# Seven more matmuls on zeros, a Hankel tile loaded in half the partitions, and an earlier load of the output weights, in a fused attention and max-out feed-forward kernel

## The chip, the cores and the metric

The kernel runs on one core of one Trainium2 chip. The metric is the time of one execution in microseconds (us), as the device reports it. Three runs of the kernel before gave 312.24, 312.76 and 314.45 us; the median is 312.76 us.

## What is computed

Two operations are chained. The first is attention with a relative position bias, for 8 batches of 8 heads, 576 positions and 64 channels for each head. The second is a feed-forward block on the 4608 tokens of 512 channels that the attention gives. Its middle layer of 768 takes the largest of three products.

```python
scores = scale * np.matmul(q, k.transpose(0, 1, 3, 2))
bias = bias_table[bucket]                     # bucket depends on |i - j| alone, capped at 128
attn = softmax(scores + bias)                 # over the keys
x = (attn @ v) as 4608 tokens x 512           # heads side by side
h = np.maximum(np.maximum(x @ w1, x @ w2), x @ w3)
out = h @ w_out
```

## The kernel before, in words

**Units of work.** A batch has 576 positions: four tiles of 128 and a tail of 64. Heads are taken in pairs (`hp`, four pairs in a batch), since two heads of 64 channels fill 128 partitions. Queries are taken in two halves (`c` is 0 for queries 0 to 255, and 1 for 256 to 511), with the tails of queries and keys handled apart (`left_queries`, `left_keys`). For a pair, `scores` multiplies keys by queries into a PSUM tile `sc`, and ScalarE takes the exponential into `e4` in SBUF. The bias enters as a factor: `times_band` multiplies the part of `e4` that lies near the diagonal by a tile `hank` on VectorE. `attend` multiplies the result by the values `vx` (whose last column is ones, so that it gives the sums too), and its `quotients` divides on VectorE into `x_sb`. `x_sb` is transposed into `xT`, from which the feed-forward products are taken.

**The Hankel tile.** `spread_bias` makes, for each of the 8 heads, a row of 511 factors in `w_sb`, writes it to DRAM (`w_dr`), and `load_hank` reads it back so that partition p gets the row from element p on: 384 elements for each head, in two DMAs of four heads. `bandt` is a copy of a part of it for the tails.

**Order.** Nearly everything on TensorE, VectorE and ScalarE is put down in program order (`inorder`, with the helpers `mm`, `tr`, `dve_copy`, `act_copy`), so the order of the source lines is the order in each engine's queue. Feed-forward work waits in a list `pending` and is put between attention pieces by `fill`, in portions; `first`, `second` and `third` are the products with w1, w2 and w3 and are called `f`, `m` and `g` in the lists, and `o` is the output product with `wo_bf`.

**The first batch.** It is started by hand. Queries and keys come in as 32-bit values on the SP and ACT queues, or cast by DMA on the POOL queue, and are transposed on TensorE (`first_transposes` for keys and the first 256 queries, `more_transposes` for the other queries, `last_keys` for the key tails of pairs 0 and 1). While loads are on their way, TensorE multiplies a block of zeros: eight times at the very start (`warm`) and once in each head pair of the first half (`keep_warm`, tile `idle`). A first loop over `hp` does the first half of the queries of all four pairs, with the bands of pairs 0 and 1 at its end. A second loop does the other half, the attends, and the first feed-forward portions.

**The POOL queue.** All casting loads go through it, in program order: queries, keys and values of the first batch, w1, then in `load_second` the second batch and w2, the second batch's values, w3, then queries and keys of batch 2 (counted from 0), its values, the output weights `wo_bf`, and queries and keys of batch 3. Each such DMA also waits until the DMA eight places ahead of it has landed, since eight semaphores are used in turn. From batch 2 on, queries and keys are transposed by DMAs on the SP queue.

**Lines.** All matmuls have line 107 in the profile and all TensorE transposes line 111, since helpers record them; VectorE copies have 124, ScalarE copies 121, exponentials 777, band products 771, `w_sb` 306, the Hankel loads 313. A group is told apart by its tiles.

Of the kernel before, what the change touches and what calls it, by code (L numbers as in the profile page):

```python
# [39 lines left out]
def kernel(  # L40
# [12 lines left out]
    nc = tc.nc  # L53
# [52 lines left out]
    def mm(*args, **kw):  # L106
        made = inorder(nc.tensor.matmul(*args, **kw))  # L107
        return made
# [14 lines left out]
    def dve_copy(out_, in_):  # L123
        return inorder(nc.vector.tensor_copy(out_, in_))  # L124
# [22 lines left out]
    def in_turn(b, load):  # L147
        return inorder(load)
# [39 lines left out]
    def go_behind(loads, behind):  # L188

        for load in loads if behind else ():  # L190
            tc.add_manual_dep(
                load.ins, behind.ins.name,
                mybir.DependencyInfo(mybir.DependencyClass.Sync, mybir.DependencyReason.DATA),
                reason="these loads go behind the transposes in line",
            )

    def load_v(b, h0, h1, behind=None):
        loads = load_main(v, b, h0, h1, vx[b % 2][:, :, :, 0:D]) + load_tail(v, b, h0, h1, v_diag)
        go_behind(loads, behind)
        return loads[-1]  # L200
# [88 lines left out]


    warm = ps_s.tile([P, 2 * CH], F32, tag="sc", name="warm")
    for _ in range(8):
        mm(warm[:, 0:CH], lhsT=zeros[:, 0:P], rhs=zeros[:])

    act_copy(batch[0][0][:, 0:2, 0:2, :], q32[:, :, 0:2, :])
    w_sb = stage.tile([H, WL], BF16, name="w_sb")

    def spread_bias():
        spread = ps_a.tile([H, NW], F32, tag="a", name="spread")
# [7 lines left out]
        inorder(nc.scalar.dma_start(out=w_dr[:], in_=w_sb[:]))  # L307

    w_dr = dram.tile([H, WL], BF16, name="w_dr")
    hank = const.tile([P, H, BAND], BF16, name="hank")  # L310

    def load_hank(h0, h1):
        inorder(nc.sync.dma_start(
            out=hank[:, h0:h1, :],
            in_=bass.AP(
                tensor=w_dr.tensor, offset=w_dr.offset + h0 * WL,
                ap=[[1, P], [WL, h1 - h0], [1, BAND]],
            ),
        ))

# [43 lines left out]
    def ffn(t0, nt, last, tiled=False):  # L366
# [268 lines left out]
        if per == 1:  # L635
            portions = [[f[0], m[0]]]
            for fb in range(1, n_fb):
                portions.append([g[fb - 1], f[fb], m[fb]])
            portions.append([g[-1], (0, None), o[0]])
        else:  # L640
            if not t0:
                portions = [[f[0]], [m[0], f[1]], [m[1]], [f[2], m[2]]]
                deferred.append(([[g[0]], g[1:]], [[x] for x in o]))
                o = []
            else:
                portions = [x for gs, _ in deferred for x in gs]
                for fb in range(n_fb):
                    portions += [[f[fb], m[fb]], [g[fb]]]
                portions += [x for _, os in deferred for x in os] + [[o[0]]]
                o = o[1:]  # L650
# [61 lines left out]
    def first_transposes(hp):  # L712


        hs = slice(2 * hp, 2 * hp + 2)
        tp = ps_f.tile([P, 2 * CH], BF16, tag="ff", name="tp1")
        K, L = KT * P, KT * P + P
        tq = tp[:, L:] if hp else ps_f.tile([P, 2 * CH], BF16, tag="ff", name="tq1")
        for t in range(2):
            tr(tq[:, P * t : P * t + P], batch[0][0][:, t, hs, :].rearrange("p h d -> p (h d)"), ident[:])  # L720
        for t in range(KT):
            tr(tp[:, P * t : P * t + P], batch[0][1][:, t, hs, :].rearrange("p h d -> p (h d)"), ident[:])
        e = K if hp < 2 else L
        if e > K:
            tr(tp[:, K:L], ktail[0][:, hp, :], ident[:])
        dve_copy(qk[0][0][:, hp, 0:QS], tq[:, 0:QS])
        dve_copy(qk[0][1][:, hp, 0:e], tp[:, 0:e])
# [83 lines left out]
    def visit(qT, kT, e4, c, mid=None, el=None):  # L811

        if el is not None:
            banks = [ps_a.tile([P, KT * 64], F32, tag="a", name="scq") for _ in range(2)]
            turn_left_queries(qT, kT, banks)
            put_left_queries(el, banks)
        for tt in range(0, KT, 2):
            scores(qT, kT, e4, c, tt)
            if tt == 0 and mid:
                mid()  # L820
# [182 lines left out]
    cast_keys(0)  # L1003
    spread_bias()
    first_transposes(0)
    for h0 in (0, KT):
        load_hank(h0, h0 + KT)
    dve_copy(batch[0][0][:, 0:2, 2:KT, :], q32[:, :, 2:KT, :])
# [20 lines left out]
        load_v(1, 0, H)  # L1029
        load_w(2)  # L1030

    def load_last_weights(behind):
        load = in_turn(0, nc.gpsimd.dma_start(out=wo_bf[:], in_=moe_w_out.rearrange("(c p) m -> p c m", p=P)))
        go_behind([load], behind)

    def bands(hp):
        for t in range(KT):
            times_band(hp, first_e[hp], t, 0, QS, inorder)

    def keep_warm():  # L1040

        idle = ps_a.tile([P, CH], F32, tag="a", name="idle")
        mm(idle[:], lhsT=zeros[:, 0:P], rhs=zeros[:])


    first_e, lefts = [], []
# [1 line left out]
    for hp in range(HP):  # L1048
        qT, kT = (x[:, hp, :] for x in qk[0])
        e4, el = e_tiles()  # L1050
        first_e.append(e4)
        visit(qT, kT, e4, 0, (lambda: first_transposes(hp + 1)) if 0 < hp < HP - 1 else None)
        if hp == HP - 1:
            more_transposes(0)
        if hp == 0:
            first_transposes(1)
        if hp == 1:
            last_keys()
        if hp + 2 < HP:
            cast_keys(hp + 2)  # L1060
        if hp == HP - 1:
            bands(0)
            bands(1)
        late.append(lambda hp=hp, e4=e4, el=el: attend(0, hp, e4, el, 0))
        keep_warm()
        lefts.append(lambda hp=hp, qT=qT, kT=kT, el=el: left_keys(
            hp, qT, kT, el, 0, QS, ps_a.tile([P, QS], F32, tag="a", name="sct")
        ))
        while hp and lefts:
            lefts.pop(0)()  # L1070
# [9 lines left out]
    for hp in range(HP):  # L1080
        qT, kT = (x[:, hp, :] for x in qk[0])
        if begun:
            e4, el = begun.pop()
            more_transposes(hp + 1)
            scores(qT, kT, e4, 1, 2)
        else:
            e4, el = e_tiles()
            visit(qT, kT, e4, 1, (lambda: more_transposes(hp + 1)) if hp + 1 < HP else None)

        def keys():  # L1090
            left_keys(hp, qT, kT, el, QS, S)

        def queries():
            left_queries(hp, qT, kT, el)

        def late_bands(hp=hp, e4=e4):
            for t in range(KT):
                times_band(hp, e4, t, QS, QM, inorder)

        if hp == 0:  # L1100
            keys()
        if hp == 1:
            x_transposes(0, 0)
        quotients = next_late()
        if hp < 2:
            if hp == 0:
                make_bandt()
            quotients()
            if hp == 0:
                bands(2)  # L1110
            else:
                behind.pop()()
                keys()
            queries()
            if hp == 1:
                x_transposes(1, 0)
            else:
                begun.append(e_tiles())
                scores(*(x[:, 1, :] for x in qk[0]), begun[0][0], 1, 0)
            quotients = next_late()  # L1120
            quotients()
            if hp == 0:
                bands(3)
            behind.append(lambda late_bands=late_bands, hp=hp, el=el: (late_bands(), products(hp, el)))
        else:
            if behind:
                behind.pop()()
            if hp == 3:
                quotients()
                add_ffn(0, QS)  # L1130
                fill(8)
            keys()
            if hp == 2:
                quotients()
            queries()
            late_bands()
            if hp == 2:
                x_transposes(2, 0)
                x_transposes(3, 0)
            else:  # L1140
                batch[2] = load_tiles()
                load_qk(2)
                x_transposes(0, 1)
                fill(8, lambda: second_transposes(qk[1], 0))
            products(hp, el)
        late.append(lambda hp=hp, e4=e4, el=el: attend(0, hp, e4, el, 1))

    turned = [lambda hp=hp: x_transposes(hp, 1) for hp in range(1, HP)]
    for b, hp in [(b, hp) for b in range(1, B) for hp in range(HP)]:
# [132 lines left out]
        if hp == 1 and b > 1:  # L1282
            pending.extend((n, [fn]) for n, fn in rest)
            rest.clear()
            made, tail = ffn((b - 1) * CH, CH, False, [(b + (i + 2) // HP, (i + 2) % HP) >= ROWS for i in range(HP)])
        if hp == 2 and b + 1 < B:
            last_v = load_v(b + 1, 0, H, turned_qk[b + 1, 1, min(b, 2) if b < 4 else KT - 1])
            if b == 1:
                load_last_weights(turned_qk[2, 1, KT - 1])
                batch[3] = load_tiles()  # L1290
                load_qk(3, turned_qk[2, 1, KT - 1])
        if hp == 2 and 1 < b < B - 2:
# [73 lines left out]
```

## Time and profile before

| what | value |
|---|---|
| median of three runs | 312.76 us (312.24 to 314.45) |
| profiled execution | 312.26 us, of which 310.5 us lie between its first and last instruction |
| TensorE matmuls (PE) | busy 298.9 us, 96% of the span |
| ScalarE (ACT) | 202.4 us, 65% |
| VectorE (DVE) | 207.7 us, 67% |
| GpSimd (POOL) | 110.9 us, 36%, nearly all of it issuing DMAs |
| granted TensorE clock, mean | 0.989 |
| DMA | 40.48 MB in 163950 packets |

How to read it: times are from the start of the span. A row of the timeline has the start, the duration, the engine, the source line, the operation with its output and input tiles and shapes, a count, and in brackets how long the engine sat idle before and what ended the wait. A row of the table of windows has the bounds in us, the length, and for each engine the busy time and the number of instructions, then the granted TensorE clock (1.00 is full), the busy share of the DMA engines and GB/s. A DMA's landing is counted from its issue.

### The profile page before, as it was taken

What the parts mean: (1) busy time and instruction counts of PE and PEld (TensorE: products, weight loads), DVE (VectorE), ACT (ScalarE), POOL (GpSimd) and SP (SyncE); (2) the same over time, 40 slices, a digit from 0 to 9 for tenths busy, and PEclk for the clock granted to TensorE, in tenths of its full rate; (3) what the DMA queues carried; (4) which work ended last, traced back from release to release, by engine and by line L of the source; (5) the groups of instructions that cost most, each with busy time, mean ns of one, the idle gap of its engine ahead of it and who ended that gap; (6) DMA issues with size and microseconds to landing.
All of it is one profiled execution on the core that took longest, in us unless ns stands there. A gap on an engine that the chain in (4) does not pass through costs nothing.

```text
span 310.5 us, 10532 instructions
## 1 busy us (share of the span) xinstructions
PE 298.9 (96%) x4542; PEld 182.5 (59%) x4542; DVE 207.7 (67%) x475; ACT 202.4 (65%) x268; POOL 110.9 (36%) x147
## 2 busy tenths in 40 slices
PE   6989999999999999999999999989999999999995
PEld 2357777775555655657665756666667654444442
DVE  7389788776777776776777667766776665553552
ACT  3899988886778777767776877675776730122211
POOL 8978752951096008900647024901500000000000
PEclk9599999999999999999999999999999999999999
DMA  9999999999999999999999999999932014202003
GB/s 167 198 187 199 182 163 136 145 166 139 141 157 191 151 187 155 133 147 198 105 101 125 165 183 111 112 146 202 131 62 106 36 33 80 101 0 103 34 0 135
DMA packets 163950, 40.48 MB, mean 130 GB/s; under 512 B 153784, under 2 KB 159424, under 8 KB 163904
## 3 DMA queue, kind: packets, MB, share of 16 engines
q0 software_dynamic: 103840, 16.66, 75.7%
q1 hardware_dynamic: 58304, 22.69, 43.6%
q8 instruction: 35, 0.57, 0.8%
q10 hardware_dynamic: 1760, 0.47, 0.7%
q14 instruction: 11, 0.09, 0.1%
HBM read 35.39 MB, written 9.45 MB: 144 GB/s over the span
## 4 chain that ended last, share of the span: by engine, by line
PE 89%; ACT 5%; DMA 2%; issue 1%; DVE 1%; ACTq 1%; DVEq 0%
PE psp L107 34%; PE ps L107 19%; PE a L107 14%; PE sc L107 9%; PE pso L107 6%; ACT e L777 4%; PE sct L107 2%; PE scq L107 2%; PE tp L111 1%; DMA xT<-in_q_dram 1%; DMA out_dram<-osb 1%; ACT el L777 1%; ACTq L213 1%; PE xp L111 0%; DVE k_sb L124 0%
## 5 line engine op out<-in xcount | busy, mean ns | idle before, releaser
L777 ACT ACTIVATE e<-sc 128x1024 bf16<-128x1024 f32 x128 | 128.4, 1023 | 30.4 <-PE sc L107 27.3
L107 PEld LDWEIGHTS <-w_bf 64*128 64x128 bf16 (+1 forms) x1088 | 73.4, 95 | 57.9 <-issue 5.0
L107 PE MATMUL psp<-xT,w_bf 64*128 64x512 bf16 x736 | 91.9, 376 | 1.9 <-issue 1.8
L771 DVE TENSOR_TENSOR e<-e,hank 128x512 bf16<-128x512 bf16 (+2 forms) x136 | 62.3, 473 | 20.3 <-ACT e L777 19.7
L107 PE MATMUL ps<-xT,w_bf 128*128 128x512 bf16 (+1 forms) x352 | 65.6, 336 | 0.0
L153 POOL DMA_DIRECT2D vx<-in_v_dram x28 | 24.7, 895 | 83.0 <-DMA kT<-k_sb 40.7
L107 PE MATMUL sc<-qT,kT 64*128 64x256 bf16 (+1 forms) x384 | 48.6, 312 | 2.0 <-DVE kT L124 0.8
L107 PEld LDWEIGHTS <-kT 64*128 64x128 bf16 (+1 forms) x736 | 31.3, 95 | 26.8 <-issue 8.4
L107 PE MATMUL a<-vx,e 64*128 64x65 bf16 (+1 forms) x1536 | 44.7, 191 | 0.0
L107 PEld LDWEIGHTS <-e 64*128 64x128 bf16 (+1 forms) x1536 | 40.7, 95 | 3.7 <-issue 0.2
L107 PEld LDWEIGHTS <-hT 64*128 64x128 bf16 (+1 forms) x444 | 26.9, 95 | 19.4 <-DVE hT L519 1.9
L107 PE MATMUL a<-vt,el 64*128 64x65 bf16 (+1 forms) x240 | 30.8, 201 | 0.4 <-DVE m L484 0.4
L107 PEld LDWEIGHTS <-el 64*128 64x128 bf16 (+1 forms) x624 | 26.2, 95 | 7.9 <-issue 4.7
L394 ACT ACTIVATE m<-ps 128x512 bf16<-128x512 f32 x14 | 8.4, 597 | 34.3 <-PE ps L107 34.3
L777 ACT ACTIVATE el<-sct 128x576 bf16<-128x576 f32 (+2 forms) x36 | 21.6, 603 | 13.5 <-PE sct L107 13.1
L107 PE MATMUL psp<-wo_bf,hT 64*128 64x256 bf16 (+1 forms) x336 | 29.7, 307 | 0.0
L181 POOL DMA_DIRECT2D q_sb<-in_q_dram x24 | 22.1, 921 | 10.7 <-issue 4.6
L181 POOL DMA_DIRECT2D k_sb<-in_k_dram x24 | 22.0, 917 | 4.0 <-DMA wo_bf<-in_moe_w_out_dram 2.1
L107 PE MATMUL pso<-wo_bf,hT 128*128 128x512 bf16 (+2 forms) x108 | 23.2, 367 | 0.0
L777 ACT ACTIVATE el<-scq 128x512 bf16<-128x512 f32 (+1 forms) x33 | 19.2, 585 | 3.3 <-PE scq L107 3.2
L403 DVE TENSOR_TENSOR m<-ps,m 128x512 bf16<-128x512 f32 x14 | 9.7, 692 | 17.0 <-PE ps L107 17.0
L519 DVE TENSOR_TENSOR hT<-psp,m 128x1024 bf16<-128x1024 f32 x12 | 14.7, 1225 | 6.9 <-PE psp L107 6.9
(82 smaller groups left out, 287.6 us busy)
## 6 DMA issues: line engine op xcount, KB each, us to landing
out_dram<-osb SPq DMA_DIRECT2D x35, 256.0 KB, 2.8
vx<-in_v_dram POOLq DMA_DIRECT2D x28, 128.0 KB, 5.0
q_sb<-in_q_dram POOLq DMA_DIRECT2D x26, 128.0 KB, 7.6
k_sb<-in_k_dram POOLq DMA_DIRECT2D x24, 128.0 KB, 7.8
w_bf<-in_moe_w_dram POOLq DMA_DIRECT2D x3, 768.0 KB, 9.3
xT<-in_k_dram SPq DMA_DIRECT2D x6, 128.0 KB, 4.2
hank<-w_dr SPq DMA_DIRECT2D x2, 384.0 KB, 5.7
wo_bf<-in_moe_w_out_dram POOLq DMA_DIRECT2D x1, 768.0 KB, 8.8
```

The costliest lines, as they stand in the source:

```text
L107: made = inorder(nc.tensor.matmul(*args, **kw))
L111: inorder(nc.tensor.transpose(*args))
L153: in_turn(b, nc.gpsimd.dma_start(out=dst[:, t, h0:h1, :], in_=x[:, t, h0:h1, :])) for t in range(t0, t1)
L181: loads.append(in_turn(b, nc.gpsimd.dma_start(out=dst[:, t], in_=main_part(src, b)[:, t])))
L213: inorder(eng.dma_start(out=dst[:, :, h, :], in_=main_part(src, 0)[:, 0:nt, h, :]))
L394: nc.scalar.activation(out=st[fb]["m0"][:], in_=ps0, func=ACTF.Copy)
L403: inorder(nc.vector.tensor_tensor(out=m[:], in0=ps1, in1=st[fb]["m0"][:], op=ALU.max))
L519: return lambda: inorder(nc.vector.tensor_tensor(out=hT[:, fb * CH : fb * CH + 2 * CH].rearrange("p (i t) -> p i t", i=2), in0=ps2(), in1= ...
L771: put(nc.vector.tensor_tensor(out=e4[:, t, :, lo:hi], in0=e4[:, t, :, lo:hi], in1=hank[:, 2 * hp : 2 * hp + 2, c0:c1][:, :, ::-1], op=ALU. ...
L777: made = nc.scalar.activation(out=out_, in_=in_, func=ACTF.Exp, scale=inv_sqrt_d)
```

## The change

It joins several edits. (1) Seven matmuls on zeros are added: a ninth at the start, one between the first transposes and the first scores, one more in pairs 0, 1 and 3 of the first loop, and two in pair 0 of the second loop. (2) In the first loop the transposes of pair 2 come after the scores of pair 1 and no longer between their two halves. (3) In the first feed-forward portions, the second block's w1 product comes ahead of the first block's w2 product. (4) The Hankel tile is loaded into 64 partitions only, with 448 elements for each head, and two VectorE copies fill the other 64 partitions from it. The tile is 64 elements wider for each head, and `w_sb` now lies in a part of `xT` that is unused at that time. (5) The load of the output weights comes ahead of the third batch's values on the POOL queue, and no longer waits for a transpose of that batch.

```diff
-    for _ in range(8):
-        mm(warm[:, 0:CH], lhsT=zeros[:, 0:P], rhs=zeros[:])
+    def on_zeros(out_, n=1):
+        for _ in range(n):
+            mm(out_, lhsT=zeros[:, 0:P], rhs=zeros[:])
+
+    on_zeros(warm[:, 0:CH], 9)
...
-    w_sb = stage.tile([H, WL], BF16, name="w_sb")
+    w_sb = xT[0:H, 0, 3 * CH + P : 3 * CH + P + WL]
...
-    hank = const.tile([P, H, BAND], BF16, name="hank")
+    hank = const.tile([P, H, BAND + 64], BF16, name="hank")
...
-            out=hank[:, h0:h1, :],
+            out=hank[0:64, h0:h1, :],
...
-                ap=[[1, P], [WL, h1 - h0], [1, BAND]],
+                ap=[[1, 64], [WL, h1 - h0], [1, BAND + 64]],
...
+    def copy_hank(h0, h1):
+        dve_copy(hank[64:, h0:h1, 0:BAND], hank[0:64, h0:h1, 64:])
...
-                portions = [[f[0]], [m[0], f[1]], [m[1]], [f[2], m[2]]]
+                portions = [[f[0]], [f[1], m[0]], [m[1]], [f[2], m[2]]]
...
     first_transposes(0)
+    on_zeros(warm[:, 0:CH])
...
-    def load_last_weights(behind):
-        load = in_turn(0, nc.gpsimd.dma_start(out=wo_bf[:], in_=moe_w_out.rearrange("(c p) m -> p c m", p=P)))
-        go_behind([load], behind)
+    def load_last_weights():
+        in_turn(0, nc.gpsimd.dma_start(out=wo_bf[:], in_=moe_w_out.rearrange("(c p) m -> p c m", p=P)))
...
-    def keep_warm():
+    def keep_warm(n):
...
-        mm(idle[:], lhsT=zeros[:, 0:P], rhs=zeros[:])
+        on_zeros(idle[:], n)
...
-        visit(qT, kT, e4, 0, (lambda: first_transposes(hp + 1)) if 0 < hp < HP - 1 else None)
+        visit(qT, kT, e4, 0, (lambda: first_transposes(hp + 1)) if hp == 2 else None)
...
-        if hp == 0:
-            first_transposes(1)
+        if hp < 2:
+            first_transposes(hp + 1)
...
         if hp == HP - 1:
+            copy_hank(0, KT)
             bands(0)
             bands(1)
+            copy_hank(KT, H)
...
-        keep_warm()
+        keep_warm(1 if hp == 2 else 2)
...
         if hp == 0:
+            keep_warm(2)
             keys()
...
         if hp == 2 and b + 1 < B:
+            if b == 1:
+                load_last_weights()
             last_v = load_v(b + 1, 0, H, turned_qk[b + 1, 1, min(b, 2) if b < 4 else KT - 1])
             if b == 1:
-                load_last_weights(turned_qk[2, 1, KT - 1])
                 batch[3] = load_tiles()
```

## The prediction

> **What bounds the kernel now.** I read first the shares of the page: TensorE 96%, so a gain must give TensorE less idle or less slow time. The clock row of the page (9599...) has one low slice near the start, and all edits touch the first 70 us. So next I read windows around that slice, with bounds 3.41 us apart, since that spacing puts the low clock exactly into two of them.
>
> ```profile
> 4.07:7.48 3.41, 2.28 (x20) 0.88 (x18) 2.75 (x11) 1.64 (x5) 3.41 (x6) 1.00 1.57 210
> 7.48:10.89 3.41, 2.89 (x20) 1.37 (x20) 1.48 (x6) 2.69 (x3) 3.41 (x5) 0.50 2.08 179
> 10.89:14.30 3.41, 3.41 (x23) 1.37 (x22) 1.46 (x5) 2.71 (x4) 3.41 (x6) 0.50 1.22 208
> 14.30:17.71 3.41, 2.62 (x27) 1.23 (x26) 1.78 (x7) 3.37 (x6) 2.19 (x4) 1.00 2.09 181
> ```
>
> TensorE runs at half clock from 7.48 to 14.30. The window ahead of it has 2.28 us of matmul (67%); the one after, 2.62 us (77%), isn't followed by a drop. ACT is busy 2.7 of 3.41 us in the two slow windows and 3.37 in the next. Its timeline shows what the slow clock costs: three waits for scores, then a chain without a gap.
>
> ```profile
> 9.68 1.02 ACT L777 ACTIVATE e<-sc 128x1024 bf16<-128x1024 f32 x1 [0.53 <-PE sc L107]
> 11.08 1.02 ACT L777 ACTIVATE e<-sc 128x1024 bf16<-128x1024 f32 x1 [0.38 <-PE sc L107]
> 12.18 0.66 ACT L777 ACTIVATE el<-sct 128x256 bf16<-128x256 f32 x2
> 12.94 1.02 ACT L777 ACTIVATE e<-sc 128x1024 bf16<-128x1024 f32 x1
> 14.34 1.02 ACT L777 ACTIVATE e<-sc 128x1024 bf16<-128x1024 f32 x1 [0.38 <-PE sc L107]
> ```
>
> The chain of work that ended last agrees: PE and DVE up to 14.34, ACT exponentials to 18.72, then PE and ACT in turn, and PE nearly alone from 26.1 on. In the timeline VectorE sits idle 1.63 us before 16.12, then works almost without a gap to 30.8. Last I read which DMAs bound the way down.
>
> ```profile
> 17.36 0.70 POOL L223 DMA_DIRECT2D xT<-in_k_dram  x1 [1.22 <-DVE e L771]
> 20.74 0.79 POOL L1014 DMA_DIRECT2D w_bf<-in_moe_w_dram  x1
> 32.23 0.76 POOL L1014 DMA_DIRECT2D w_bf<-in_moe_w_dram  x1 [0.75 <-DMA xT<-in_k_dram]
> 57.96 0.85 POOL L1033 DMA_DIRECT2D wo_bf<-in_moe_w_out_dram  x1 [0.50 <-DMA kT<-k_sb]
> ```
>
> From issue to landing, w2 (20.74) and w3 (32.23) take 9.3 us each, so they land at 30.0 and 41.5; wo (57.96) takes 8.8 and lands at 66.8. In PE's timeline their first users start at 30.07, 41.87 and 68.62. So the slack is 0, 0.4 and 1.8 us: who speeds up the start runs into them. The key-tail transpose of batch 2 (issued 55.40, 6.0 to land: 61.4) has 0.9 us to its user at 62.31.
>
> **What the Trainium skill says.** "TensorE: Matmul & The Clock Gate", Part 1, has the clock at full or half only, set by how busy TensorE was in a free-running window of about 3.4 us, whose phase differs from run to run. The trace agrees: 0.50 for 6.82 us, two windows. The same page ("Wait — 56ns, not 53.3ns?") prices a 512-column matmul at 426.7 ns at half clock and 215.7 at full; here the starting zeros' weight loads are 0.43 us apart. "VectorE: DVE Perf Modes", the tier table, gives a bf16 SBUF copy the 4x rate; the trace agrees (64x768 in 350 ns, 128x512 in 279). "DMA: Bandwidth & Descriptors", "Queues, rings and completion order", says that an engine goes round between the queues that have work. The trace agrees: the first two value loads of batch 0, issued 0.76 us apart, land after 4.4 and 6.7 us, at 13.8 and 16.9; the Hankel loads (issued 10.01 and 10.38, landing after 5.2 and 6.2 us) lie between them. Later value loads land 0.3 to 0.5 us apart.
>
> **The change part by part.**
>
> *Zeros and order (1, 2).* Seven matmuls, 0.22 us each at full clock. Two fall into the window before the drop, into gaps in which TensorE waits for VectorE (0.47 us before 4.97, 0.52 before 6.52): they cost nothing and lift it from 2.28 to 2.71 us, 79%, over the 77% that was followed by full clock. So I take it that the clock stays up at 7.48. From there, step by step: pair 1's key transposes end 0.2 us earlier (0.39 instead of 0.60 us), its scores take 0.39 instead of 0.61, so its first exponential starts at 9.27 and not 9.68. Pair 1's second scores no longer stand behind seven transposes. ACT then runs at its own pace: 0.92 us for each exponential (1.83 for two, in the chain), 0.28 for each tail. 9.27 + 2 x 0.92 + 2 x 0.28 = 11.67; pair 2 to 13.51, its tail 13.79, pair 3 to 15.63. Before, pair 3's ended at 17.47. **ACT is 1.84 us ahead.** Moved transposes: pair 2's are 0.2 us of scores later, yet full clock ends them at 9.9 instead of 10.4. Inputs are there: queries' later tiles land by 11.1, tails by 11.6. The zeros after 8 us sit where TensorE waits for a VectorE copy or for ACT (0.80 us before 18.72); without that cover, five cost 1.1 us, at half clock 2.1.
>
> *Hankel tile (4).* Each DMA has 256 packets of 896 B instead of 512 of 768. By packets half is saved, by bytes 42%. The two hold back the value loads by 3.1 us less 0.5, so 2.6; saved, about 1.2 (bounds 0 and 1.5). The tile should land by about 14 instead of 15.2. VectorE gets two copies of 64x1536: 0.35 + 768 x 0.071/256 = 0.56 us each, **1.1 in all** (0.9 if they pipeline, 1.9 at half rate). Queued behind the first are pair 0 and 1's bands; behind the second the copy of queries for pair 1, bandt and the first quotients. VectorE's stretch from 16.12 starts at 14.15 (pair 3's scores at 13.9, plus transposes 0.25): copy of queries 0.24, Hankel 0.5, bands 1.74, Hankel 0.5, queries 0.24, bandt 0.71 bring it to 18.1, where before the quotient started at 19.65 after 0.60 us of waiting. **VectorE is 1.5 us ahead**, less than ACT, and becomes what the attends wait for (their slack to VectorE was 0.1 us at 24.63 and 27.44). So 1.5 us is what reaches 28 us. `w_sb` inside `xT` costs nothing: no wait is added for it.
>
> *Order of w1 and w2 (3).* With PE 1.5 us ahead the old order would stand 1.5 us at w2. A w1 product (0.98 us, 8 matmuls) and ten transposes (0.56) now go first, and w2 itself lands earlier, as the value loads let POOL issue earlier (17.36 moves to about 16.2). Cost 0; the one ScalarE copy (0.60) that moves ahead of the key copies fits in ACT's 0.55 us gap at 31.71.
>
> *w3, not edited.* Needed at 41.87 - 1.5 = 40.4, landing at 41.5 less the 1.2 of the lighter Hankel loads: 40.3. No stall; 1.1 us if nothing is saved.
>
> *Output weights (5).* Issued at about 45.7, after batch 2's key tails, ahead of four value loads and two tail loads, which wait for a transpose until 52.68 anyway. It lands near 55 instead of 66.8; the user comes at 67.1, so an order as before would just do: worth 0 to 0.3 us. In return 0.77 MB share the DMA engines with batch 2's transposes. These are paced by SP (1.2 to 1.7 us each, ten of them), so I take 0; the other bound is 0.6 us at 62.31.
>
> **Sum** against the profiled execution: 312.26 - 1.5 = 310.8 us (310.5 of span and 1.8 around it). The median of three is 0.5 higher, with a spread of 2.2 us that the phase of the window may make; I take 0.3 of it: **311.1 us**.
>
> **The rivals.** *Forecast, 0.60:* 310.1 (ACT's 1.84 and the output weights' 0.3, no offset) to 311.9. *A, the lead is eaten further down, 0.20:* w3 or the key-tail transpose arrives as before, or VectorE's copies take 0.95 each. For it: slack of only 0.4 and 0.9 us. Against: the 3.1 us hole in the value loads. 312.26 - 0.4 = 311.9, median about 312.3. *B, slower, 0.12: the drop comes later.* TensorE now finishes its first-half work early and waits for ACT, so a window after 10.9 may fall under the mark[...]. Two slow windows in 17.7 to 24.5, where PE is busy 6.1 of 6.8 us, lose 3.4 us less 0.7 of idle: 2.7. 312.26 - 1.5 + 2.7 = 313.5, with the median's offset 313.8. *C, the clock still drops at 7.48, 0.08:* the zeros don't do what they are there for; they cost about 0.4 us at half clock against 0.3 us from the order: 312.8.
>
> **The numbers.** The likeliest is 311.1. From 310.1 to 313.5 all cases but the worse half of B and a tail of luck are held. 1% is 3.1 us, and about what a measurement of this kernel can tell from no change: faster by that needs 309.6, more than ACT's whole lead of 1.84 gives, 0.03; slower needs 315.9, B with more than two windows, 0.03.
>
> **What would show it.** Clock 1.00 in all windows after the first 4 us; pair 3's second exponential ending near 15.6; the second value load landing before 16; VectorE's first quotient near 18.1; no wait for w_bf in PE's weight loads; the first output product near 67. I am wrong if a slow window stands later, or if the 1.5 us of 28 us is not found at 68.

## The result, and the profile after

The kernel after took 316.83 us (median of 22 runs, 313.18 to 319.7), the kernel before beside it 313.33 us (22 runs, 310.42 to 321.7). The ratio is 1.0093, interval 1.0071 to 1.0115: the change costs 0.93%, 2.9 us by the ratio. Medians here count all runs; a ratio leaves out the runs more than 1.5% above the fastest of their kernel (7 of the 22 of after), so it can lie below the ratio of the medians. Forecast were 311.1 us and a gain. The profiled execution of after took 314.74 us, with a span of 313.0; that of before 312.26 and 310.5. So the profile shows 2.5 us of the loss.

Windows of after, with the bounds used for before (columns as described ahead of the prediction):

```profile
4.07:7.48 3.41, 3.11 (x16) 1.00 (x16) 2.22 (x11) 1.37 (x4) 3.41 (x6) 1.00 1.54 202
7.48:10.89 3.41, 2.79 (x35) 1.52 (x31) 1.46 (x6) 3.08 (x4) 3.41 (x5) 1.00 2.09 182
10.89:14.30 3.41, 2.71 (x25) 1.05 (x24) 1.78 (x6) 3.00 (x5) 3.41 (x6) 1.00 1.52 157
14.30:17.71 3.41, 2.79 (x23) 1.24 (x23) 2.33 (x6) 3.41 (x7) 3.41 (x6) 1.00 2.18 158
```

The half clock from 7.48 to 14.30 is gone, as forecast. (The first 1.00 isn't the whole truth: time of which the profile has no record counts as full in this column. In PE's timeline of after the product that spreads the bias takes 1.01 us at 5.15, where before had 0.59 us at 4.97, so TensorE still ran at half clock there, and opened near 6.5 us.) Yet the start is no faster where it counts. The timelines of ScalarE and of VectorE in after, and behind them before's first quotient:

```profile
7.81 3.77 ACT L784 ACTIVATE e<-sc 128x1024 bf16<-128x1024 f32 x4 [0.61 <-PE sc L107]
...
14.61 1.99 ACT L784 ACTIVATE e<-sc 128x1024 bf16<-128x1024 f32 x2
```
```profile
15.24 0.32 DVE L124 COPY qT<-tp 128x320 bf16<-128x320 bf16 x1 [1.63 <-PE tp L111]
15.60 0.96 DVE L124 COPY hank<-hank 64x1536 bf16<-64x1536 bf16 x1
16.66 1.83 DVE L778 TENSOR_TENSOR e<-e,hank 128x512 bf16<-128x512 bf16 x6
18.52 0.76 DVE L124 COPY hank<-hank 64x1536 bf16<-64x1536 bf16 x1
...
20.47 0.18 DVE L919 RECIPROCAL rd<-a 128x4 f32<-128x4 f32 x1
```
```profile
19.65 0.18 DVE L912 RECIPROCAL rd<-a 128x4 f32<-128x4 f32 x1 [0.60 <-PE a L107]
```

Pair 3's exponentials end at 16.60, 0.9 us ahead of before (17.48) and not 1.84. VectorE's first quotient starts at 20.47, 0.8 us late, and was to be 1.5 early. Then the stretch that moved the output weights. The DMA queues of GpSimd and of SyncE in after, and two rows of SyncE's before:

```profile
31.77 0.75 POOL L1022 DMA_DIRECT2D w_bf<-in_moe_w_dram  x1 [0.97 <-DMA xT<-in_k_dram]
45.09 0.86 POOL L1041 DMA_DIRECT2D wo_bf<-in_moe_w_out_dram  x1
57.17 3.52 POOL L153 DMA_DIRECT2D vx<-in_v_dram  x4 [11.22 <-PE sct L107]
```
```profile
48.06 3.12 SPq L709 DMA_TRANSPOSE qT<-q_sb  x1
51.23 1.26 SPq L709 DMA_TRANSPOSE kT<-k_sb  x1
52.58 3.30 SPq L709 DMA_TRANSPOSE qT<-q_sb  x1
55.98 1.22 SPq L709 DMA_TRANSPOSE kT<-k_sb  x1
57.29 1.20 SPq L709 DMA_TRANSPOSE qT<-qtail  x1
58.59 1.22 SPq L709 DMA_TRANSPOSE kT<-ktail  x1
```
```profile
51.00 1.23 SPq L702 DMA_TRANSPOSE qT<-q_sb  x1
...
55.40 1.21 SPq L702 DMA_TRANSPOSE kT<-ktail  x1
```

The output weights are in flight from 45.09 to 56.1 (11.0 us to land). In that time two transposes hold SP's queue for 3.12 and 3.30 us; the same queue before had 1.2 to 1.7 us for each. The key tails' transpose is issued at 58.59, 3.2 us later than at 55.40. TensorE meets it (timeline of PE, after, then before):

```profile
64.69 0.42 PE L107 MATMUL sct<-qT,kT 128*128 128x512 bf16 x2 [1.80 <-DMA kT<-ktail]
```
```profile
62.31 0.41 PE L107 MATMUL sct<-qT,kT 128*128 128x512 bf16 x2
```

Before, there was no wait. The first output product starts at 70.95 (68.62 before): the weights themselves were never late in either kernel.

The quotients on VectorE are the mile posts for what follows: the start of a quotient in one profile less that of the same quotient in the profile of before. For after this is +0.82 us at 19.65 us of before's time, +0.42 at 41.95, +0.43 at 62.16, **+2.39 at 65.49**, and +2.47 at 253. Nearly the whole loss of the profiled execution is the wait for the key tails.

Single profiles scatter, though. The unchanged kernel, profiled again, stands +2.1 us at 253. So the ratios below, from many runs, carry the verdicts on time, and the profiles only say which waits there are. What the profile of after doesn't show is a second loss. In 8 of its 22 runs the mean clock is 0.997 or more (median 315.62 us); in the other 14 it is 0.992 to 0.995 (317.94), about one closed window (a window in which the clock falls back to half). The profiled one is of the first sort.

### The profile page after: what moved, and what is told of

The parts are those of the page before. It is cut to its first block, busy times and chain, and to the rows that moved or that the text cites. A ratio compares the mean times of both kernels' runs of the same rounds, so it can differ in the third digit from the quotient of the medians.

```text
span 313.0 us, 10548 instructions
## 1 busy us (share of the span) xinstructions
PE 299.3 (96%) x4549; PEld 181.8 (58%) x4549; DVE 209.2 (67%) x477; ACT 202.3 (65%) x268; POOL 110.9 (35%) x147
## 4 chain that ended last, share of the span: by engine, by line
PE 82%; SPq 5%; DVE 4%; ACT 4%; DMA 3%; issue 2%; ACTq 0%; DVEq 0%
PE psp L107 33%; PE ps L107 17%; PE a L107 12%; PE sc L107 7%; PE pso L107 6%; SPq L709 5%; ACT e L784 2%; PE sct L107 2%; DMA kT<-ktail 2%; DVE e L778 2%; PE warm L107 1%; PE scq L107 1%; ACT el L784 1%; DMA out_dram<-osb 1%; PE tp L111 1%
## 5 line engine op out<-in xcount | busy, mean ns | idle before, releaser
L778 DVE TENSOR_TENSOR e<-e,hank 128x512 bf16<-128x512 bf16 (+2 forms) x136 | 61.4, 466 | 19.5 <-ACT e L784 18.9
L107 PE MATMUL sc<-qT,kT 64*128 64x256 bf16 (+1 forms) x384 | 47.3, 306 | 2.7 <-ACT e L784 1.1
L107 PEld LDWEIGHTS <-kT 64*128 64x128 bf16 (+1 forms) x736 | 30.6, 94 | 29.9 <-issue 8.7
L121 ACT ACTIVATE m<-psp 128x1024 bf16<-128x1024 f32 (+1 forms) x22 | 18.2, 826 | 3.1 <-PE psp L107 3.1
```

The source lines that it names most:

```text
L121: return inorder(nc.scalar.activation(out=out_, in_=in_, func=ACTF.Copy))
L778: put(nc.vector.tensor_tensor(out=e4[:, t, :, lo:hi], in0=e4[:, t, :, lo:hi], in1=hank[:, 2 * hp : 2 * hp + 2, c0:c1][:, :, ::-1], op=ALU. ...
```

## The experiments

The theories at the start: (L) the lead of the first 28 us is real but is taken by the loads that bound the way down; (W) the output weights hold back the transposes of batch 2; (H) the Hankel copies cost VectorE more than their lighter loads give. The rival: (K) the clock, which closes later or at another place.

**The output weights.** The first run has the whole change with only this edit undone, the second this edit alone on the kernel before:

```diff
         if hp == 2 and b + 1 < B:
+            if b == 1:
+                load_last_weights()
             last_v = load_v(b + 1, 0, H, turned_qk[b + 1, 1, min(b, 2) if b < 4 else KT - 1])
             if b == 1:
-                load_last_weights(turned_qk[2, 1, KT - 1])
```

The third has the whole change, but the weights, ahead of the values, still wait for a transpose (`load_last_weights` taking `behind` again):

```diff
-                load_last_weights()
+                load_last_weights(turned_qk[2, 1, KT - 1])
             last_v = load_v(b + 1, 0, H, turned_qk[b + 1, 1, min(b, 2) if b < 4 else KT - 1])
```

> The changed kernel with the load of the output weights back behind batch 2's values and its last transpose; all else as changed. Theory (the early output weights hold up batch 2's transposes on the shared DMA engines): the key-tail transpose is issued near 55 and not 58.6, TensorE doesn't wait for it (1.8 us in the changed kernel), and the time falls by about 1.8 us from the changed kernel, to about 0.6 us above the kernel before. Rival (the key-tail wait comes from the later start or from the wider Hankel tile): the wait stays at 1 us or more and the time stays within 0.5 us of the changed kernel.

> The kernel before with only the load of the output weights moved ahead of batch 2's values, not waiting for a transpose. Theory: transposes of batch 2 are held up by about 3 us, TensorE waits about 1.5 to 2.3 us for the key tails near 62, the time rises by about 2 us. Rival: no wait, within 0.3 us of the kernel before.

> The changed kernel, with the output weights still ahead of batch 2's values on the POOL queue but waiting for batch 2's last tile transpose as before. Theory (what costs is that their transfer lies beside the transposes, not their place in the queue): no long wait for the key tails near 62, and about the time of the run in which both place and wait were put back, 315.6, or above it where the values, now behind, come late. Rival (the place in the queue costs): the wait for the key tails stays at 1 us or more.

Alone, the edit costs 0.66% (315.37 us, ratio 1.0066, 1.0045 to 1.0087). The timeline of PE with that edit alone:

```profile
63.80 0.42 PE L107 MATMUL sct<-qT,kT 128*128 128x512 bf16 x2 [1.22 <-DMA kT<-ktail]
```

Its key-tail transpose was issued at 58.48. That place sorts all 17 profiles of this study: in the three whose weights go out at about 45 us it is issued at 58.48 to 58.59, in the fourteen others at 55.30 to 57.06. With the edit undone on the changed kernel the transpose came at 55.79 and the wait was 0.30 us, but the time fell only from 316.83 to 315.63 us; in ratios from 1.0093 to 1.0077 (1.0055 to 1.0099), and these two intervals overlap. So W is shown by the edit alone and by the transposes' times; that undoing it gains time isn't shown, and W is not all.

With the old wait kept, nothing waits for key tails, but the weights (issued at 57.04) now stand ahead of the values (57.87), and these come late. Time 321.4 us, ratio 1.0205 (1.0148 to 1.0262; 6 runs). Timeline of PE and a window of that kernel:

```profile
72.54 0.27 PE L107 MATMUL a<-vt,el 128*128 128x130 bf16 x1 [5.63 <-DMA vt<-in_v_dram]
```
```profile
74.00:76.00 2.00, 2.00 (x28) 1.59 (x26) 0.93 (x4) 0.04 (x1) 1.08 (x3) 0.50 1.98 148
```

The clock reads 0.82, 0.50, 0.50, 0.50 and 0.97 in the five stretches of 2 us from 70 to 80: the stall of 5.63 us closes it for 6.8 us, two windows. The quotients' offset goes from -0.02 before it to +8.28 after both.

**The Hankel tile.** First undone in the kernel after, then done alone on the kernel before:

```diff
-            out=hank[:, h0:h1, :],
+            out=hank[0:64, h0:h1, :],
...
-                ap=[[1, P], [WL, h1 - h0], [1, BAND]],
+                ap=[[1, 64], [WL, h1 - h0], [1, BAND + 64]],
...
         if hp == HP - 1:
+            copy_hank(0, KT)
             bands(0)
             bands(1)
+            copy_hank(KT, H)
```

> The changed kernel with the Hankel tile loaded into all 128 partitions by DMA and no VectorE copies; all else as changed, the early output weights too. Theory (the two copies, 0.96 and 0.76 us, put VectorE 0.8 us behind the kernel before at the first quotients): first quotient near 19 instead of 20.5, TensorE at the second batch's first scores about 1 us earlier than in the changed kernel, but the lead is then eaten by the key-tail wait, so the time falls by less than 0.5 us. Rival (the copies lie beside other work): the second batch's first scores start where they start in the changed kernel, 33.1.

> The kernel before with only the Hankel tile in 64 partitions and the two copies. Theory: VectorE's first quotient comes about 1.3 us later than before (19.65), the time rises by 0.7 to 1.3 us. Rival (what the lighter DMAs give back pays for the copies): within 0.3 us of the kernel before; the second value load lands near 14 and not 16.9.

Alone it gave 314.02 us, ratio 1.0028 (1.0003 to 1.0053). VectorE in that run:

```profile
17.91 0.55 DVE L124 COPY hank<-hank 64x1536 bf16<-64x1536 bf16 x1
...
20.43 0.76 DVE L124 COPY hank<-hank 64x1536 bf16<-64x1536 bf16 x1
```

The first quotient came at 22.38, 2.73 us late, but not through the copies alone: in this profile TensorE ran at half clock up to near 17 us (four key transposes take 0.63 us at 14.15; at full clock 0.39). It is also the slowest of its 22 runs (316.21 us), and such an offset is not their rule. The tile landed 5.5 and 6.6 us after issue, no sooner than before (5.2 and 6.2); in the kernel after it was 4.7 and 5.4. Without the Hankel edit the changed kernel has its first quotient 1.48 us early, which is the forecast's number; but at 44.85 the offset is -0.62 and at 65.49 +1.57. It waits 0.90 us for the w3 weights and 1.27 us for the key tails. Its time is 317.1 us (1.0121, 1.009 to 1.0152; 6 runs), no better than the whole change. Compare profiles with the clock at full from 6.5 to 20 us: the first quotient comes at 19.80 to 20.47 in the three with the copies (20.23 on the mean), at 18.17 to 18.70 in the seven without (18.40). So H is shown for the start of VectorE, 1.8 us, about what the two copies take; its cost in time is barely clear of nothing (the interval begins at 1.0003), and L takes what its undoing gives.

**Orders, zeros, and both.** On the kernel before: the two orders alone (the diff); the seven zeros alone, as in the change; both together; and nothing at all.

```diff
-                portions = [[f[0]], [m[0], f[1]], [m[1]], [f[2], m[2]]]
+                portions = [[f[0]], [f[1], m[0]], [m[1]], [f[2], m[2]]]
...
-        visit(qT, kT, e4, 0, (lambda: first_transposes(hp + 1)) if 0 < hp < HP - 1 else None)
+        visit(qT, kT, e4, 0, (lambda: first_transposes(hp + 1)) if hp == 2 else None)
...
-        if hp == 0:
-            first_transposes(1)
+        if hp < 2:
+            first_transposes(hp + 1)
```

> The kernel before with only the two orders (pair 2's transposes behind pair 1's scores; the second block's w1 product ahead of the first block's w2 product). Theory: a third exponential without a wait, a lead of 0.3 to 0.9 us at the first quotient, part of it kept at 60 us, the end within 0.5 us of the kernel before. Rival (the orders are what slows the joined kernel): 1 us or more above the kernel before.

> The kernel before with only the seven added matmuls on zeros. Theory now (the clock drop at 7.5 us costs nothing: in the runs of the kernel before, those with a mean clock below 0.990 have the same times as those at 1.0; the ninth zero at half clock delays the start by 0.4 to 0.6 us): time 0 to 0.6 us above the kernel before, first quotient no earlier than before. The prediction's theory (a held clock lets the exponentials run 1.5 us ahead): 1 to 1.5 us below the kernel before.

> The kernel before with the zeros and the two orders, without the Hankel tile and the output weights. Theory (a lead of the start, here 1.5 us at 25 us as in the run with the Hankel tile put back, is taken away by loads that come when they came before: w3 near 41.5, batch 2's transposes near 60): a lead of over 1 us at 25 us, PE waits for w3 of about 0.9 us, end within 0.7 us of the kernel before. Rival (the lead lasts): 1 us or more below the kernel before.

> The kernel before, unchanged, as if it were a change: what the comparison tells where nothing differs, and a second profile of it. Theory (the clock drop at 7.5 us in the first profile of it is one case of several: 37 of 54 of its runs had a mean clock of 0.997 or more): ratio within 0.3% of 1, and this profile has full clock from 8 us on or a drop of its own, with the second batch's first scores up to 1.6 us earlier than in the first profile. Rival (the drop is a fixed part of the kernel before): clock 0.5 again from 7.5 to 14.3.

The orders alone: 313.81 us, 0.9994 (0.997 to 1.0018), no difference. Their profile shows how a lead goes. The first quotient is 1.16 us early, and at 41.95 still 1.08; then TensorE's timeline has

```profile
42.15 1.05 PE L107 MATMUL ps<-xT,w_bf 128*128 128x256 bf16 x8 [1.20 <-DMA w_bf<-in_moe_w_dram]
```

and the offset is +0.25, and 0.00 at 62.16. The w3 weights arrive when they did before.

That lead isn't the orders' own, though. The run with the output weights alone, whose start is that of before, has the whole lead that was forecast. ScalarE, VectorE and TensorE's weight loads in it:

```profile
13.69 1.99 ACT L777 ACTIVATE e<-sc 128x1024 bf16<-128x1024 f32 x2
```
```profile
18.46 0.18 DVE L912 RECIPROCAL rd<-a 128x4 f32<-128x4 f32 x1
```
```profile
29.63 0.77 PEld L107 LDWEIGHTS <-w_bf 128*128 128x128 bf16 x8 [0.96 <-DMA w_bf<-in_moe_w_dram]
```

Pair 3's exponentials end at 15.68 (forecast 15.63), the first quotient is 1.19 us early, and the lead goes at w2: the offset is -1.64 at 29.15, -0.45 at 34.48 and -0.41 at 62.16. What the orders do is to move this loss: with them TensorE waits for w2 0.25 us at most, and the lead lasts to w3.

The zeros alone: first quotient 1.30 us early, 0.60 after a wait of 0.75 us for w2, 0.25 at 44.85, and then a wait of 1.29 us for the key tails, though the output weights weren't moved; time 316.14 us, 1.0053 (1.0024 to 1.0082). Zeros and orders: the same loss of the lead to w3 (1.18 us), no wait for key tails, but one near 100 us:

```profile
101.25 0.22 PE L107 MATMUL a<-vt,el 128*128 128x130 bf16 x1 [3.28 <-DMA vt<-in_v_dram]
```

The clock reads 0.87, 0.50 and 0.78 in the three stretches of 2 us from 100 on: one closed window after the stall, which takes the offset from +3.52 to +5.01. Time 316.88 us (1.0049, 1.0006 to 1.0092). That wait is not the change's own: the unchanged kernel profiled again (313.21 us, ratio 1.0001, 0.998 to 1.0021) waits 1.66 us at the same values. It has no drop at 7.48 to lose: TensorE hasn't left half clock by then. Timeline of PE in it:

```profile
8.28 0.63 PE L111 MATMUL tp<-ident,k_sb 128*128 128x128 bf16 x4
...
12.69 0.39 PE L111 MATMUL tp<-ident,k_sb 128*128 128x128 bf16 x4
```

The clock opened near 10.6 us, and still the first quotient is 0.63 us early; at 62.16 it is 0.31.

These transposes tell the starts of all 17 profiles apart. Between 7 and 9 us pair 1's four take 0.39 or 0.40 us, full clock, in all seven profiles of kernels with the two zeros at the start, and in the one with forty. Of the nine with eight zeros there as before, six have 0.60 to 0.63 us: five opened late, at 10 to 17 us, and in the first profile of before the clock had fallen back. So the zeros at the start very likely do what they are for. But the clock at 7.48, on which the prediction built, is worth little: the two other profiles with before's start, without that drop, are only 0.41 us (the output weights alone, opened near 5 us) and 0.31 us (this one) ahead at 62.16.

The mean clock of a run doesn't show this, as it counts the time before the first record as full; it counts windows that close later. Of the 205 runs of before that stood beside these experiments, 145 have 0.997 or more (median 313.4 us), and 18 less than 0.990, about two closed windows, like the first profile of before: 313.8 us, a difference within the scatter.

**Is the lead to be had if w3 comes sooner?** The two orders again, with w3's load ahead of batch 1's values:

```diff
-        load_v(1, 0, H)
         load_w(2)
+        load_v(1, 0, H)
```

> The kernel before with the two orders, and the load of w3 ahead of batch 1's values on the POOL queue. Theory (w3's arrival at 41.5 to 42.2 us takes the lead of the start away): no wait for w3, the lead of about 1 us at 35 us still there at 60, the time 0.5 to 1 us below the kernel before, unless the key tails of batch 2 take it at 62. Rival (the lead is taken there anyway, by the values that now come later): no better than the two orders alone, within 0.3% of the kernel before.

It gave 314.16 us (1.0011, 0.9992 to 1.0029), no gain. The wait for w3 is gone, but PE's timeline has another in its place:

```profile
42.21 0.23 PE L107 MATMUL a<-vt,el 128*128 128x130 bf16 x1 [1.27 <-DMA vt<-in_v_dram]
```

In this run the queue brought only one of the two in time. It had no lead to lose (+0.16 at its first quotient; the clock opened near 13 us), so what an early w3 would do for one that has it wasn't seen.

**Why do zeros cost anything?** All on the kernel before: first the two at the start alone (the ninth, and the one after `first_transposes(0)`), then the five later ones alone:

```diff
-        keep_warm()
+        keep_warm(1 if hp == 2 else 2)
...
         if hp == 0:
+            keep_warm(2)
             keys()
```

Then these five with 64 columns in place of 512, and ten in place of five. The last kernel has 32 short ones more behind the eight at the start:

```diff
+    for _ in range(32):
+        mm(warm[:, 0:64], lhsT=zeros[:, 0:P], rhs=zeros[:, 0:64])
```

> The kernel before with only the two zeros ahead of the first scores (the ninth and the one behind the first transposes). Theory (what the zeros cost is the delay of the start, since the ninth runs at half clock wherever the clock opens late): 0.4 to 1.7 us above the kernel before, as with all seven. Rival (the later five cost): within 0.3% of the kernel before.

> The kernel before with only the five zeros in the head pairs. Theory as for the two at the start: within 0.3% of the kernel before. Rival: 1 to 1.7 us above it.

> The kernel before with five matmuls on zeros added at the five later places, as in the run of the later zeros (1.0039, 1.0017 to 1.0062), but each of 64 columns in place of 512. They multiply no data that the result uses. Theory time: the five cost TensorE time that no wait covers, five times 0.22 us; with 64 columns that is five times 0.03 us, so 1.000 (0.999 to 1.001). Theory blocks: not their time but their number counts, since ten more instructions (five weight loads, five matmuls) stand ahead of every later one, and the stalls of TensorE without a releaser near 178 and 210 us fall on other work and get longer: 1.003 to 1.004, as with the long ones, and stalls of about 3.3 us in sum between 175 and 220 us in place of 2.2.

> The kernel before with ten matmuls on zeros of 512 columns added at the five later places, twice as many as in the run of the later zeros. They multiply no data that the result uses. Theory time: twice the cost of five, 2.4 us, 1.008 (1.005 to 1.011). Theory blocks: 1.002 to 1.005, no more than with five, since only the place of the stalls moves; what the waits at the start cover is free.

> The kernel before with 32 matmuls on zeros of 64 columns more at the very start, 64 more instructions on TensorE; the start becomes longer by 2 to 3.5 us, which isn't asked. Asked is where TensorE's waits without a releaser near 178 and 210 us lie. Theory blocks: they stay at the same number of TensorE instructions from the start (5535 to 5543 and 6812 to 6820 records of matmuls and weight loads), so at work that stands 64 instructions earlier in the program. Theory place: they stay at the same work, at 5600 and 6876 records.

| zeros added to the kernel before | median, us | ratio |
|---|---|---|
| two at the start | 313.8 | 1.001 (0.9987 to 1.0034) |
| five later | 314.8 | 1.0039 (1.0017 to 1.0062) |
| five later, 64 columns | 314.72 | 1.0052 (1.0025 to 1.0078) |
| ten later (6 runs) | 319.26 | 1.0126 (1.0063 to 1.0188) |

The short ones cost as much as the long ones, so the theory of TensorE's own time falls for the five. In their profile with 512 columns the offset is -0.17 as late as 172 us; the loss (to +1.40) lies between there and 222 us, mostly at two stalls for which the profile shows no releaser. The last kernel tells where these lie. Timeline of PE, and a window that ends just before the first stall:

```profile
178.95 0.61 PE L107 MATMUL sc<-qT,kT 64*128 64x512 bf16 x2 [3.12 <-issue]
...
213.03 0.70 PE L107 MATMUL psp<-wo_bf,hT 64*128 64x256 bf16 x9 [1.73 <-issue]
```
```profile
0.00:178.90 178.90, 167.15 (x2763) 109.08 (x2772) 127.25 (x337) 135.69 (x184) 92.17 (x124) 1.00 1.66 157
```

Ahead of the stall stand 2763 matmuls and 2772 weight loads: 5535 records, as in the other kernels (5534 to 5543 in fifteen of them, with 0 to 20 instructions added), and ahead of the second 6813 (6811 to 6820). With 64 instructions more at the start the stall is at the same count, so at work 64 instructions earlier in the program. Had it belonged to certain work, it would stand at 5600. In this run it also closed the clock: 0.50 from 179 to 182 us. That points to blocks of instructions (last section): added instructions move the borders of the blocks onto other work. In the eight profiles of kernels with five to seven long zeros or the two at the start, the stalls without a releaser between 175 and 225 us sum to 3.3 us on the mean; in the six without zeros to 2.2. That is of the size of the five's cost, 1.2 us, but the scatter from profile to profile is as large (1.3 to 3.5 us without zeros, 2.1 to 5.2 with), with the short zeros it was 2.5, and with ten only 2.2. So: that the cost of the five doesn't come from their time on TensorE is shown. What it comes from isn't: the block borders may be it, but so may the places, or the PSUM tile that the pair in the second loop takes, in all these runs, from a pool of two that other work uses in turn. The two at the start, without such a tile, cost nothing that shows. The ten came out above what either theory had. Their profile has a wait of 5.13 us for values near 103 us with a closed window after it, and four of the six runs have a mean clock of 0.992 to 0.995. The interval holds what the theory of time expected (1.008), so on ten it decides nothing.

No kernel of these was shown to be faster than the kernel before.

## Why the prediction was wrong

**The clock.** That the zeros keep it up at 7.48 held, and seven profiles against nine make it likely that they are the reason. The step that failed is the next one: that the half clock before costs the kernel 1.5 us, so that removing it gains them. In my sum this lead was the only term that wasn't nothing. The kernel with only the output weights moved had an open clock and the forecast lead without any zero or new order, and kept 0.41 us of it behind w2. I took one profile of before for the rule, in which the clock had opened near 4 us and fallen back; in its second profile it opened near 10.6. I had cited that the window's phase differs from run to run, and used it to place the windows and not to ask what the start is worth in other phases.

The reason that I gave for the clock, the share of matmul time in a window (67% was followed by a drop, 77% wasn't), doesn't hold as a mark. In the profile with the short zeros a window with 1.89 us of matmul in 3.41 (55%, 7.54 to 10.95) is followed by half clock and one with 1.56 (46%, 208.92 to 212.33) by full clock; in before itself one with 2.24 (66%, 208.86 to 212.27) is followed by full clock. The step from 67 to 79% was right by luck.

**"ACT is 1.84 us ahead"** came out as 0.9. The first exponential started at 7.81 instead of 7.21, 0.6 us late, since the clock opened later than in the profile of before and the spread of the bias took 1.01 us and not 0.59. That isn't the zeros' doing: with nine of them and an earlier clock (the output weights undone) it started at 7.26, with before's eight and a later clock (before's second profile) at 7.78. Of the 0.6 us at most 0.2 are the ninth zero's (spread at 5.15 and not 4.97). I had reckoned all of after's start with the clock as it opened in one run.

**"VectorE is 1.5 us ahead"** came out as 0.8 late, 2.4 from the forecast 18.1. Its stretch began at 15.24 and not 14.15 (1.1 us: pair 3's transposes follow scores that waited for ACT), and lasted 5.2 us instead of 3.9. Most of that is the two Hankel copies: 0.96 and 0.76, 1.72 in sum, where I took 1.0 in the chain and named 1.9 as the bound. The tile, forecast for 14, landed at 15.5: 4.7 us after an issue (10.81) that came 0.8 us later than before. The lighter loads gave less than the 1.2 us taken: the w3 load was issued at 31.77 for 32.23, 0.46 us. The second value load landed 3.2 us after issue in place of 6.7, but that took 4.6 us in before's second profile and 5.9 with the Hankel edit alone, so it can't be credited to the lighter loads. All this mattered less than it seems, since without the Hankel edit the 1.5 us were there at 19 us and gone by 45.

**Rival A, "the lead is eaten further down"**, is what happens to whatever lead there is. That the old order of w1 and w2 would stand at w2, and the new one wouldn't, I had right. In the runs with orders, zeros or both and in the changed kernel without the Hankel edit, 0.35 to 1.3 us of it went at w3 between 42 and 45 us. I had the slack right (0.4 us) and gave the rival 0.20, because I let the Hankel saving pay for w3.

**The output weights** are the second step that failed, a term that I put at nothing. I took 0 and named 0.6 us as the other bound at 62.31. Measured: 1.80 us of wait in after, 1.22 alone, 0.66% of time alone, 2.1 us by the ratio. (Some wait at this place can come without the edit: 1.29 us with the zeros alone.) My reason, that the transposes are paced by SP's queue and so not by the DMA engines, is what failed. SP's pace is itself a matter of DMA: two transposes went from 1.2 to over 3 us on its queue while 0.77 MB were cast beside them. The weights, too, took longer to land: 11.0 us instead of 8.8. I had cited that a DMA engine goes round between the queues that have work, and used it for the Hankel loads and not here.

**Rival B, a later drop of the clock,** was right in kind and wrong in cause. I had it come from TensorE finishing early and being less busy. In the four profiles that show one between 20 and 300 us it follows a wait of TensorE of over 3 us, for values in three and for a block of instructions in one; where I followed it, it cost 1.5 and 2.6 us on top of the wait. 14 of the 22 runs of after have a mean clock that fits one closed window, and lie 2.3 us above the others. Behind which wait it falls there stays open.

**The sum.** The single edits cost 0.53 (zeros), -0.06 (orders), 0.28 (Hankel) and 0.66% (output weights), 1.4 in all, against 0.93 joined. The four intervals allow 0.5 either way in the sum, so whether the parts add isn't decided.

## What to carry to other kernels

A lead at the start of a kernel is worth what the tightest load after it leaves: list the issue, landing and first use of every load on the way, and add the lead only up to the smallest slack. Ahead of moving a large load forward, look at what other queues do in the 10 us of its flight, DMA transposes above all, because a queue's pace is no cover if its own items are DMAs. And profile the kernel before twice: a slow window or a wait that is missing in the second profile is no place to gain. Read the clock of the start from the matmuls' own times too, not from the clock column alone.

## What the runs showed of the hardware

*Stalls at borders of instruction blocks.* TensorE waits with no releaser at fixed counts of its instructions. In one profile with four such waits, the records ahead of them are 5535, 5791, 6812 and 7068: 256 apart in both pairs, and 5 x 256 less 3 between the first of each (some records are missing). The page of after shows the queue that fits:

```profile
PE 299.3 (96%) x4549; PEld 181.8 (58%) x4549; DVE 209.2 (67%) x477; ACT 202.3 (65%) x268; POOL 110.9 (35%) x147
...
DMA  9999999999699999997999999999942013202003
...
q8 instruction: 35, 0.57, 0.8%
```

The two counts of 4549 make 9098 instructions, 35.5 blocks of 256; the queue moved 35 packets of 16 KB. "Runtime: NRT & Kernel Launch" in the Trainium skill ("Instruction fetch mechanics") gives refills of 16 KiB, 256 instructions, by DMA, and calls a border's cost mostly hidden. The size agrees. Hidden they mostly are, too: of 35 borders two to four show in a profile. But where they show, they cost 0.2 to 3.1 us each, and the DMA engines are then nearly full (the row of tenths). That the block comes late because of this load is my reading; it wasn't tried.

*How long a stall closes the clock.* TensorE waits of up to 2.70 us left the clock at full; 3.12, 3.28 and 5.13 us closed it for about one window, 5.63 us for two (6.8 us). "TensorE: Matmul & The Clock Gate" ("Why this matters for your kernels") names gaps of over about 3 us, and these waits agree. The drops ahead of 20 us in two of the profiles came without such a gap.

*When the clock opens.* TensorE starts at half clock (the starting zeros are 0.43 us apart), and by the times of its matmuls it reached full clock anywhere from near 4 to near 17 us in the 17 profiles, by 6.5 us in all seven with nine zeros at the start.

*A copy from one half of the partitions to the other* of 64 x 1536 bf16 took VectorE 0.55 to 0.96 us for the same instruction in the kernel after and in the one with the Hankel edit alone.
